# Outer gate taken as a per-token scale in the output evacuation, with exp of its logit folded into attention, and gate logits in four column tiles

## The chip, the cores and the metric

The kernel runs on one core of a Trainium2 chip. The metric is the device time of one execution in microseconds (us). Engines are named PE (TensorE matmul; PEld is its weight loading), DVE (VectorE), ACT (ScalarE), POOL (GpSimd) and SP (SyncE, which here only issues DMAs).

## The reference

```
x = A_x                                             # 2048 tokens x 512
g = sigmoid((x * gate_w).sum(-1, keepdims=True))    # one number per token
a = attention(x)     # 32 heads of 16, 4 segments of 512 tokens: causal softmax inside a
                     # segment, mixed with a linear-attention memory (phi, M, z) of the
                     # earlier segments by sigmoid(beta) per head; then @ wo
b = (gelu(x @ w_gate) * (x @ w_up)) @ w_down        # hidden size 1792
return g * a + (1 - g) * b
```

## The kernel before

The whole program is a list of tasks (`add`, `group`, `evac`), each with an engine (or a choice of two), a guessed cost, a priority and the tasks it depends on. A planner (`Sched.run`) walks through time with those guesses and emits the instructions of each engine in the order in which it would start them. The order on each engine is therefore fixed when the program is built, and a changed cost, dependency or task anywhere can move instructions that the edit does not mention, and can move an evacuation from DVE to ACT or back. `group` makes a PE task that fills a PSUM tile; `evac` makes the task that empties it. PSUM tiles come from two rings: "lg" (three tiles of 128x1024, for gate pairs and attention logits) and "gen" (two tiles of 128x512, for everything else). The planner also knows PE's tile modes: "row" (attention logits, four heads in four row strips), "col" (attention times values, four column strips) and "full". It charges 100 ns for a mode change and holds a "col" group back for up to 2.2 us unless a "row" group went just before it.

The work has two parts. The first, up to about 80 us, loads the weights, computes q, k and v of segment 0, and all the gate products of the geglu: `gate_pair` (28 of them, tile `gt`) multiplies x by 256 columns of w_gate and ACT applies gelu into `G`. `up_group` (56, tile `up`) multiplies by w_up, and DVE multiplies the PSUM result into `G`. Fourteen of the up groups (segment 0) lie in the first part, the others in the second. The second part is attention: 80 logit slots (`logit_slot`, tile `lg`), 160 exps on ACT, 160 causal selects on POOL, 32 products with the values (`pv_group`, tile `pv`), the memory (`phi`, `m_update`, `mem_den`, `mem_num`), and between the logit slots the fillers, among them the q, k, v of the next segment, the up groups, and `out_group`, which accumulates down projection and attention projection of 128 tokens in one PSUM tile (`dn`). After the last attention work four such groups are left to run alone.

The outer gate lives in `gate_row(s)`, once for each segment. `gwB` holds gate_w copied to 128 columns, so that four full matmuls of 512 columns (tile `gz`, line 452) give the logit of each token on all 128 partitions. ACT takes tanh of half of it (tile `th`, line 461). DVE makes from it `g1b` = 1 - g (line 464), which multiplies every pair of gate tiles after gelu (line 490), and, through a 32x32 block transpose (tile `tt`, line 469), `G2` = g with tokens on partitions (line 472). `G2` multiplies the reciprocal of the softmax sum (`f_rg`, line 665) and that of the memory's denominator (`f_g`, line 803). So g reaches the attention side and 1 - g the geglu side before both are added up in PSUM, and the evacuation of the sum (`osb`, through the helper `copy`, lines 181 and 183) is a plain copy.

The task that opens the pool of the attention tiles (`reopen`) depends on all gate pairs being multiplied and on `G2`; the pool `ph1` of the first part, which holds w_gate, `g1b`, `th` and `tt`, is closed there, and the attention tiles take its memory.

Of the kernel before, what the change touches and what calls it, by code (L numbers as in the profile page):

```python
# [8 lines left out]
AF = mybir.ActivationFunctionType  # L9
ALU = mybir.AluOpType  # L10
BF = dt.bfloat16
F32 = dt.float32

P = 128
# [141 lines left out]
def kernel(  # L156
# [22 lines left out]
    def copy(e, dst, src):  # L179
        if e == "ACT":  # L180
            nc.scalar.activation(dst, src, AF.Copy)  # L181
        else:
# [9 lines left out]
             "osb": 2, "th": 1, "tt": 1}  # L192
# [3 lines left out]
    def ctile(name, shape, dtype=BF):  # L196
        return cp.tile(shape, dtype, name=name, tag=name)
# [28 lines left out]
    gwB = ctile("gwB", [P, FC, P])  # L226
# [5 lines left out]
    G2 = ctile("G2", [P, NSEG, QB], F32)  # L232
    omg = ctile("omg", [P, NCH], F32)
# [16 lines left out]
    g1b = p1.tile([P, NSEG * L], BF, name="g1b", tag="g1b")  # L250
# [198 lines left out]
    def gate_row(s, prio):  # L449
        def mms(t):  # L450
            for fc in range(FC):
                nc.tensor.matmul(t[:, :], lhsT=gwB[:, fc, :], rhs=xT[:, fc, s * L:(s + 1) * L],
                                 start=(fc == 0), stop=(fc == FC - 1))
        gwt = TAB.get("gwB")
        g, box = group("gz", 4 * MM, mms, prio, [a_x[s], gwt])
        read_x[s].append(g)
        tl = {}

        def f_th(e, t):
            tl["th"] = rtile("th", [P, L], F32, p1)  # L460
            nc.scalar.activation(tl["th"][:, :], t[:, :], AF.Tanh, scale=0.5)

        def f_g1(e):
            nc.vector.tensor_scalar(out=g1b[:, s * L:(s + 1) * L], in0=tl["th"][:, :],
                                    scalar1=-0.5, scalar2=0.5, op0=ALU.mult, op1=ALU.add)

        def f_tt(e):
            tl["tt"] = rtile("tt", [P, QB, 32], F32, p1)
            nc.vector.transpose(tl["tt"][:, :, :].rearrange("p a b -> p (a b)"), tl["th"][:, :])

        def f_g2(e):
            nc.vector.tensor_scalar(out=G2[:, s, :], in0=tl["tt"][:, :, 0], scalar1=0.5,
                                    scalar2=0.5, op0=ALU.mult, op1=ALU.add)
        th = evac("ACT", g, box, f_th, alloc=["th"])
        g1 = add("DVE", 420, f_g1, deps=[th], prio=1, frees=[("th", th)])
        tt = add("DVE", 630, f_tt, deps=[th], prio=6, alloc=["tt"], frees=[("th", th)])
        g2 = add("DVE", 110, f_g2, deps=[tt], prio=6, frees=[("tt", tt)])
        TAB[("g1", s)], TAB[("g2", s)] = g1, g2

    def gate_pair(s, hp, prio):  # L480
        def mms(t):
# [8 lines left out]
        GM[(s, hp)] = add("DVE", 620, lambda e: nc.vector.tensor_mul(  # L490
            dst, dst, g1b[:, s * L:(s + 1) * L][:, None, :].to_broadcast((P, 2, L))),
            deps=[ge, TAB[("g1", s)]], prio=4)
# [10 lines left out]
    def f_gwB(e):  # L503
        for fc in range(FC):
            nc.vector.tensor_copy(gwB[:, fc, :], gw[:, fc:fc + 1].to_broadcast((P, P)))
    TAB["gwB"] = add("DVE", 1000, f_gwB, deps=[a_gw], prio=3)
# [26 lines left out]
    for s in range(NSEG):  # L533
        gate_row(s, 40 + 20 * s)
# [15 lines left out]
    opened = add("EXT", 0, reopen, deps=list(GM.values()) + [TAB[("g2", s)] for s in range(NSEG)])  # L550
# [71 lines left out]
    def pv_group(s, c, e):  # L622
# [58 lines left out]
        rg = add("DVE", 120, f_rg, prio=3, deps=[r, TAB[("g2", s)]])  # L681
# [185 lines left out]
    def out_group(s, qt, prio):  # L867
# [6 lines left out]
        def fn(e):  # L874
            bx["o"] = rtile("osb", [P, D])
            copy(e, bx["o"][:, :], box["t"][:, :])
        ev = add(["DVE", "ACT"], [610, 560], fn, prio=0, deps=[g], alloc=["osb"],
# [55 lines left out]
    for s in range(NSEG):  # L933
        for t in range(NSLOT):
            logit_slot(s, t)
            if TAB["first_x"] is None:
                TAB["first_x"] = XT_[(0, 0)]
            if t == 0:
                if s == 0 or True:
                    fillers(s)  # L940
# [38 lines left out]
```

## Time and profile before

| | |
|---|---|
| time, median of 3 runs | 293.13 us (293.1 to 293.29) |
| profiled execution, its own time | 292.86 us |
| its span | 291.2 us |
| PE busy | 274.3 us (94% of the span) |
| ACT busy | 210.6 us (72%) |
| DVE busy | 197.6 us (68%) |
| POOL busy | 126.5 us (43%) |
| PE clock granted | 0.999 of full speed |

The span runs from the first to the last instruction of the profiled execution; 1.66 us of its own time lie outside it. Busy time is the time in which at least one instruction of the engine is open. Matmuls are pipelined: in a stream of 512-column matmuls each lasts about 380 ns from start to end, but one starts every 216 ns.

### The profile page before, as it was taken

Reading aid. Unit: us, or ns where it says so; the run is one execution under the profiler, and the core shown is the slowest. Engines: PE = TensorE matmul, PEld = TensorE weight load, DVE = VectorE, ACT = ScalarE, POOL = GpSimd, SP = SyncE. Lnnn points to the kernel's source line nnn. Section 1 sums busy time; section 2 is a strip of 40 time slices with the busy share of each in tenths; the row PEclk is TensorE's granted clock in tenths of the full one; section 3 lists DMA queues with packets and bytes.
Section 4 is the critical chain, followed back from the end, with each engine's and each line's share of the span. In section 5 each row is a group of like instructions: output and inputs, shape, how many; then the busy total and the mean of one; then the engine's idle time right before and its main releaser. Section 6 shows DMA issues by size and latency. Waiting matters only on the chain.

```text
span 291.2 us, 5670 instructions
## 1 busy us (share of the span) xinstructions
PE 274.3 (94%) x2279; PEld 118.8 (41%) x2320; DVE 197.6 (68%) x355; ACT 210.6 (72%) x231; POOL 126.5 (43%) x188
## 2 busy tenths in 40 slices
PE   8999999999999979999998999988999999997994
PEld 3444444444434433443334444333444434333441
DVE  2331796554577898888999687699977865868400
ACT  3634664353399969899988999999998998985111
POOL 8000000000038674955478686564855864564000
PEclk9999999999999999999999999999999999999999
DMA  7975930000001130100002010000000000000011
GB/s 246 337 123 142 372 117 2 0 0 2 0 0 37 38 38 2 38 0 2 1 2 56 18 39 19 20 0 2 2 19 20 8 14 20 19 20 18 20 36 37
DMA packets 22019, 13.74 MB, mean 47 GB/s; under 512 B 14056, under 2 KB 20968, under 8 KB 21992
## 3 DMA queue, kind: packets, MB, share of 16 engines
q1 hardware_dynamic: 20392, 11.80, 14.8%
q10 hardware_dynamic: 1600, 1.57, 1.6%
q8 instruction: 18, 0.29, 0.4%
q14 instruction: 9, 0.07, 0.1%
HBM read 8.13 MB, written 2.10 MB: 35 GB/s over the span
## 4 chain that ended last, share of the span: by engine, by line
PE 73%; DVE 20%; DMA 3%; issue 1%; ACT 1%; ACTq 0%
PE gt L337 17%; PE dn L838 15%; PE up L337 14%; PE lg L582 6%; PE pv L634 6%; PE dn L843 4%; DMA wga<-in_B_w_gate_dram 3%; PE v L434 3%; PE q L337 3%; DVE T L652 3%; DVE N L670 2%; DVE G L499 2%; PE k L337 2%; DVE Nm L826 2%; DVE Tm L822 1%
## 5 line engine op out<-in xcount | busy, mean ns | idle before, releaser
L605 ACT ACTIVATE pT<-lg 128x1024 bf16<-128x1024 f32 x160 | 153.5, 1028 | 12.9 <-PE lg L582 12.3
L614 POOL TENSOR_SCALAR_AFFINE_SELECT pT<-pT 128x512 bf16<-128x512 bf16 (+1 forms) x160 | 94.3, 600 | 133.9 <-ACT pT L605 133.2
L499 DVE TENSOR_TENSOR G<-up,G 128x512 bf16<-128x512 f32 x56 | 38.3, 687 | 28.3 <-PE up L337 28.2
L337 PE MATMUL up<-xT,wup 128*128 128x512 bf16 x213 | 55.3, 380 | 1.1 <-DVE G L499 0.4
L838 PE MATMUL dn<-wdn,G 128*128 128x512 bf16 x213 | 52.3, 380 | 2.3 <-DVE T L652 1.3
L487 ACT ACTIVATE G<-gt 128x1024 bf16<-128x1024 f32 x28 | 28.7, 1024 | 33.9 <-PE gt L337 33.7
L337 PE MATMUL gt<-xT,wga 128*128 128x512 bf16 x217 | 51.3, 379 | 0.7 <-DMA wga<-in_B_w_gate_dram 0.3
L337 PEld LDWEIGHTS <-wga 128*128 128x128 bf16 x224 | 21.7, 98 | 26.8 <-DMA wga<-in_B_w_gate_dram 0.8
L838 PEld LDWEIGHTS <-G 128*128 128x128 bf16 x224 | 20.4, 98 | 27.1 <-issue 5.6
L337 PEld LDWEIGHTS <-wup 128*128 128x128 bf16 x224 | 20.0, 97 | 25.8 <-issue 5.6
L652 DVE STREAM_TRANSPOSE T<-pv 128x512 f32<-128x512 f32 x32 | 22.8, 711 | 10.9 <-PE pv L634 10.8
L490 DVE TENSOR_TENSOR G<-G,g1b 128x1024 bf16<-128x1024 bf16 x28 | 18.4, 685 | 2.1 <-ACT G L487 2.1
L181 ACT ACTIVATE osb<-dn 128x512 bf16<-128x512 f32 x9 | 5.4, 596 | 19.0 <-PE dn L843 19.0
L582 PE MATMUL lg<-qT,kO 32*128 32x128 bf16 (+2 forms) x320 | 18.1, 272 | 0.0
L582 PE MATMUL lg<-qT,kT 16*128 16x256 bf16 (+2 forms) x320 | 17.9, 273 | 0.1
L434 PE MATMUL v<-wv,xT 128*128 128x512 bf16 x61 | 15.5, 379 | 1.2 <-DVE vz_84 L183 0.5
L843 PE MATMUL dn<-wo,xT 128*128 128x512 bf16 x64 | 16.5, 380 | 0.1
L337 PE MATMUL q<-xT,wq 128*128 128x512 bf16 x60 | 15.8, 380 | 0.7 <-DVE kT L183 0.5
L582 PEld LDWEIGHTS <-kT 16*128 16x128 bf16 x320 | 7.1, 92 | 19.7 <-issue 19.2
L670 DVE TENSOR_TENSOR N<-T,r 128x512 bf16<-128x512 f32 x16 | 14.8, 926 | 0.3
L634 PE MATMUL pv<-pT,vz_84 128*32 128x256 bf16 (+2 forms) x320 | 11.7, 275 | 2.3 <-POOL pT L614 1.8
L582 PEld LDWEIGHTS <-kO 32*128 32x128 bf16 x320 | 7.1, 92 | 14.4 <-issue 14.1
(115 smaller groups left out, 270.3 us busy)
## 6 DMA issues: line engine op xcount, KB each, us to landing
out_dram<-osb SPq DMA_DIRECT2D x16, 128.0 KB, 1.7
wup<-in_B_w_up_dram SPq DMA_DIRECT2D x1, 1792.0 KB, 8.0
wdn<-in_B_w_down_dram SPq DMA_DIRECT2D x1, 1792.0 KB, 13.5
wga<-in_B_w_gate_dram SPq DMA_DIRECT2D x1, 1280.0 KB, 10.7
wq<-in_A_wq_dram SPq DMA_DIRECT2D x1, 512.0 KB
wga<-in_B_w_gate_dram ACTq DMA_DIRECT2D x1, 512.0 KB, 9.4
wv<-in_A_wv_dram ACTq DMA_DIRECT2D x1, 512.0 KB, 12.1
wo<-in_A_wo_dram SPq DMA_DIRECT2D x1, 512.0 KB, 9.1
```

The costliest lines, as they stand in the source:

```text
L337: nc.tensor.matmul(t, lhsT=W[:, fc, c0:c0 + P], rhs=xT[:, fc, s * L:(s + 1) * L], start=(fc == 0), stop=(fc == FC - 1))
L434: nc.tensor.matmul(t[:, :], lhsT=xT[:, fc, s * L + kt * P:s * L + (kt + 1) * P], rhs=wv[:, fc, :], start=(fc == 0), stop=(fc == FC - 1))
L487: ge = evac("ACT", g, box, lambda e, t: nc.scalar.activation(dst, t[:, :, :], AF.Gelu_apprx_tanh), cost=960, ring="lg")
L499: UPT[(s, hs)] = evac("DVE", g, box, lambda e, t: nc.vector.tensor_mul(G[:, s, hs, :], t[:, :], G[:, s, hs, :]))
L582: nc.tensor.matmul(A[j // 2][:, j % 2, at * P:(at + nq) * P], lhsT=l, rhs=r, start=True, stop=True, tile_position=(32 * j, 0))
L605: nc.scalar.activation(pT[(s, t, h)][:, :, :], A[h][:, :, :], AF.Exp, scale=0.25)
L614: nc.gpsimd.affine_select(out=v, in_=v, pattern=pat, compare_op=ALU.is_ge, fill=0.0, base=0, channel_multiplier=-1)
L634: nc.tensor.matmul(t[32 * j:32 * j + 32, qb * P:(qb + nq) * P], lhsT=vz[s % 2][:, kt, h * VW:h * VW + 32], rhs=pT[(s, t0 + w, j // 2)][:, ...
L652: nc.vector.transpose(TT[key][:, e, :, :].rearrange("p a b -> p (a b)"), t[:, :])
L670: nc.vector.tensor_mul(NN[key][:, :, :, :].rearrange("p a e d -> p e a d"), TT[key][:, :, :, 0:DH], RR[key][:, :, :, :].to_broadcast((P, 2 ...
L838: nc.tensor.matmul(t[:, :], lhsT=G[:, s, hs, qt * P:(qt + 1) * P], rhs=wdn[:, hs, :], start=(hs == 0), stop=stop and (hs == HS - 1))
L843: nc.tensor.matmul(t, lhsT=xT[:, c, s * L + qt * P:s * L + (qt + 1) * P], rhs=wo[:, c, :], start=first and c == 0, stop=(c == NCH - 1))
```

## The change

The sum g*a + (1-g)*b is rewritten as (1-g) * (e^z * a + b), where z is the gate's logit, since g/(1-g) = e^z. `G2` becomes e^z, and 1 - g = 1/(1 + e^z) becomes `omz`, a scale for each token that is applied where the finished sum leaves PSUM. The four `gate_row` become one `gate_rows`: `gwB` has 32 columns, and the four segments' logits are computed as four column tiles of one PSUM tile. DVE block-transposes that tile once; POOL spreads the result with 32 small copies over partitions into `G2` and `omz`; ACT takes exp of both, at a place after the first exp of attention; DVE finishes `omz`. The multiplication of `G` by `g1b` is gone, and with it `g1b`, `th` and the tanh. The task `gate_rows` is put ahead of the gate pairs of segment 3, and `reopen` now depends on the gelus and on POOL's copies.

```diff
-    gwB = ctile("gwB", [P, FC, P])
+    gwB = ctile("gwB", [P, FC, 32])
...
+    omz = ctile("omz", [P, NSEG, KT], F32)
...
-    g1b = p1.tile([P, NSEG * L], BF, name="g1b", tag="g1b")
...
-    def gate_row(s, prio):
+    def gate_rows(prio):
         def mms(t):
             for fc in range(FC):
-                nc.tensor.matmul(t[:, :], lhsT=gwB[:, fc, :], rhs=xT[:, fc, s * L:(s + 1) * L],
-                                 start=(fc == 0), stop=(fc == FC - 1))
...
+                for s in range(NSEG):
+                    nc.tensor.matmul(t[32 * s:32 * s + 32, :], lhsT=gwB[:, fc, :],
+                                     rhs=xT[:, fc, s * L:(s + 1) * L], start=(fc == 0),
+                                     stop=(fc == FC - 1), tile_position=(0, 32 * s),
+                                     skip_group_check=True)
+        g, box = group("gz", 4 * MM, mms, prio, a_x + [TAB["gwB"]], mode="col")
...
-            nc.scalar.activation(tl["th"][:, :], t[:, :], AF.Tanh, scale=0.5)
...
-            nc.vector.tensor_scalar(out=g1b[:, s * L:(s + 1) * L], in0=tl["th"][:, :],
-                                    scalar1=-0.5, scalar2=0.5, op0=ALU.mult, op1=ALU.add)
...
-            nc.vector.tensor_scalar(out=G2[:, s, :], in0=tl["tt"][:, :, 0], scalar1=0.5,
-                                    scalar2=0.5, op0=ALU.mult, op1=ALU.add)
...
+            nc.vector.transpose(tl["tt"][:, :, :].rearrange("p a b -> p (a b)"), t[:, :])
+
+        def f_sp(e):
+            z = tl["tt"]
+            for s in range(NSEG):
+                src = slice(32 * s, 32 * s + 32)
+                for j in range(4):
+                    dst = slice(32 * j, 32 * j + 32)
+                    nc.gpsimd.tensor_copy(G2[dst, s, :], z[src, :, 0])
+                    nc.gpsimd.tensor_copy(
+                        omz[dst, s, :],
+                        z[src, :, :].rearrange("p (kt a) b -> p a kt b", a=4)[:, j, :, 0])
+
+        def f_ex(e):
+            nc.scalar.activation(G2[:, :, :], G2[:, :, :], AF.Exp)
+            nc.scalar.activation(omz[:, :, :], omz[:, :, :], AF.Exp)
+
+        def f_om(e):
+            nc.vector.tensor_scalar_add(omz[:, :, :], omz[:, :, :], 1.0)
+            nc.vector.reciprocal(omz[:, :, :], omz[:, :, :])
...
+        tt = evac("DVE", g, box, f_tt, alloc=["tt"])
+        TAB["zsp"] = add("POOL", 4000, f_sp, deps=[tt], prio=6, frees=[("tt", tt)])
+
+        def later():
+            TAB["g2"] = add("ACT", 500, f_ex, deps=[TAB["zsp"], TAB["first_x"]], prio=2)
+            TAB["omz"] = add("DVE", 250, f_om, deps=[TAB["g2"]], prio=5)
...
-        GM[(s, hp)] = add("DVE", 620, lambda e: nc.vector.tensor_mul(
-            dst, dst, g1b[:, s * L:(s + 1) * L][:, None, :].to_broadcast((P, 2, L))),
-            deps=[ge, TAB[("g1", s)]], prio=4)
+        GM[(s, hp)] = ge
...
-        gate_row(s, 40 + 20 * s)
+        if s == 3:
+            gate_rows(40 + 20 * s)
...
-            copy(e, bx["o"][:, :], box["t"][:, :])
-        ev = add(["DVE", "ACT"], [610, 560], fn, prio=0, deps=[g], alloc=["osb"],
+            g = omz[:, s, qt:qt + 1]
+            if e == "ACT":
+                nc.scalar.activation(bx["o"][:, :], box["t"][:, :], AF.Copy, scale=g)
+            else:
+                nc.vector.tensor_scalar_mul(bx["o"][:, :], box["t"][:, :], g)
+        ev = add(["DVE", "ACT"], [610, 560], fn, prio=0, deps=[g, TAB["omz"]], alloc=["osb"],
```

## The prediction

> **What bounds the kernel now.** I read the busy table first, then busy time by stretch, then the chain that ended last, then single instructions.
>
> ```profile
> PE 274.3 (94%) x2279; PEld 118.8 (41%) x2320; DVE 197.6 (68%) x355; ACT 210.6 (72%) x231; POOL 126.5 (43%) x188
> ...
> 40.00:60.00 20.00, 19.89 (x92) 9.11 (x93) 12.44 (x26) 9.06 (x10) 0.00 (x0) 1.00 0.01 1
> 60.00:80.00 20.00, 19.89 (x95) 8.90 (x94) 10.75 (x18) 7.83 (x9) 0.00 (x0) 1.00 0.00 1
> ...
> 100.00:120.00 20.00, 17.26 (x176) 7.64 (x172) 18.73 (x35) 16.57 (x19) 12.91 (x17) 1.00 0.17 27
> 120.00:140.00 20.00, 19.05 (x204) 7.79 (x205) 16.79 (x29) 18.73 (x21) 12.83 (x21) 1.00 0.04 9
> 140.00:160.00 20.00, 18.07 (x212) 7.79 (x213) 19.37 (x35) 17.78 (x20) 13.88 (x19) 1.00 0.08 21
> ```
>
> The stretches give length, then PE, PEld, DVE, ACT, POOL busy. From 40 to 80 us PE is never idle while DVE and ACT are about half idle: this part is bound by PE alone, and a DVE microsecond there is worth nothing. In the second part PE, DVE and ACT are all near full, and from 100 to 120 and 140 to 160 us PE loses 2.7 and 1.9 us to DVE. The chain (start, length, what) says the same. Three pieces of it are the gate logits:
>
> ```profile
> 30.69 1.73 PE gz L452 x8
> ...
> 42.77 0.86 PE gz L452 x4
> ...
> 61.77 0.86 PE gz L452 x4
> ...
> 79.93 1.03 ACT G L487
> 80.99 0.69 DVE G L490
> 81.68 0.61 DVE G L499
> ```
>
> So the logits stand on the path with all their 3.45 us, and of the 28 multiplications of line 490 only the last stands on it. The PE sequence of the second part is what sets its end, with DVE as the engine it most often waits for.
>
> **What the Trainium skill says.** (1) "TensorE: Matmul & The Clock Gate", Part 3: matmuls in distinct column strips run concurrently; three measured 2.38 times faster. The trace agrees with more: a `pv` group is 20 matmuls in four strips, five rounds of four with 1280 columns in all per strip, and the next full matmul starts 0.67 us after the group does; its 5120 columns in turn, at 0.216 us for 512, would take 2.2 us.
>
> ```profile
> 266.89 3.18 PE L838 MATMUL dn<-wdn,G 128*128 128x512 bf16 x13 [1.30 <-DVE T L652]
> 270.00 0.73 PE L634 MATMUL pv<-pT,vz_85 128*32 128x512 bf16 x20
> 270.67 1.04 PE L843 MATMUL dn<-wo,xT 128*128 128x512 bf16 x4
> ```
>
> (2) "TensorEngine Tiling (Array Packing)", Key Properties: a change of tiling mode drains the array. The three lines price it, full to column and back. The last `dn` matmul started 0.38 us before the modelled end, 270.07; the next full one could have started 0.216 us after it, at 269.91; `pv` starts at 270.00, so entry costs 0.09. Its 1280 columns take 1280/512 x 0.216 = 0.54 of the 0.67 us, so leaving costs 0.13. Together 0.22 us. (3) "GPSIMD Engine Reference", Specifications: POOL contends with DVE instructions that have two SBUF inputs. The trace has it (start, length):
>
> ```profile
> 103.26 2.56 DVE L670 TENSOR_TENSOR N<-T,r 128x512 bf16<-128x512 f32 x1
> ...
> 103.16 2.12 POOL L708 TENSOR_TENSOR pkT<-E,Q_1013 128x1024 bf16<-128x1024 bf16 x1
> ```
>
> The 16 `N` average 0.93 us, and an undisturbed one (272.15) took 0.69.
>
> **The change part by part.**
>
> Gate logits on PE. Gone: 16 full matmuls x 0.216 = 3.46 us, all on the path. Added: 4 rounds of 4 concurrent matmuls of 512 columns, 4 x 0.216 = 0.86, plus the mode change 0.22, = 1.08 us. Gain 2.38 us. The instruction orders of the two programs show it as one block of 16 between full gate pairs, six up groups and six gate pairs before the first logit; nothing but PE's own sequence holds it. The bounds: if strips did not overlap at all, 3.46 + 0.22, a loss of 0.2.
>
> Gate multiplication and its inputs on DVE and ACT (lines 461, 464, 469, 472, 490). Gone: 28 x 0.685 = 19.2 us, 4 x 0.425, three of four transposes at 0.71 and 4 x 0.17 on DVE, 4 x 0.594 on ACT. All but the last multiplication lie beside PE work in the first part, cover being PE at 19.89 of 20 us; they are worth nothing. The last one: the second k group at 82.34 waited 0.28 us for the up evacuation behind it. The up matmuls end at 81.2 anyway, so I take 0.2, bounds 0 and 0.3. What is late next there is the table load of ACT (80.97, 1.28 us), unchanged; both programs have three.
>
> The new transpose of `gz` from PSUM: 0.71 us (the row of line 652) on a half idle DVE; nothing waits for it but POOL. The next up evacuation stands behind it, 2.6 us apart from its predecessor. Nothing.
>
> POOL's 32 copies, of 16 or 4 elements on 32 partitions. No row shows one. The nearest, a memset and a select of four elements per partition (lines 286 and 287), took 0.095 and 0.195, the select of 8x128 0.33. I take 0.2 x 32 = 6.4 us; from 3 to 11. The block of logits ends 72 matmuls (15.6 us) before the first logit slot, about 62 us, and the transpose by 63. ACT asks for `G2` after four attention activations, 5 us after its table load, about 83. That leaves 20 us, 0.6 us for each copy. POOL has nothing else to do from 20 us to there (busy 0.00), so this costs nothing; what waits behind it would be POOL's first select and ACT's exps.
>
> Two small exps on ACT, 64 and 16 elements: the activations of 1024 (1.028) and 512 elements (0.596) give 0.16 + 0.84 ns each, so 0.22 + 0.18 = 0.4 us, early in the attention. The plan moves two other evacuations from ACT to DVE there (nine left of eleven before the tail), so ACT loses 1.2 us of work against that. Two small DVE operations, 0.17 + 0.18 us (lines 518, 517). I set these at nothing net; bounds -0.4 and +0.4.
>
> Output evacuations. Same count, one scale more. Of 16, ACT did 9 and does 6, DVE 7 and now 10. The only one with no cover is the last (287.34, ACT): "ScalarE: Activation LUTs", What ACT_TABLE_LOAD costs, gives about 93 ns for each per-partition operand; the trace of before has no such activation. I take +0.09; bounds 0 and 0.1. DMAs are as before in number, size and order.
>
> Order. This is the unknown. From about 213 us on, the PE order is the same to the end. Between 80 and 213 the up groups, `pv` and memory groups stand in another order; the mode changes go from 193 to 195, both of the new ones being the logit block's. By stretches of 5 us, PE's idle time from 100 to 215 us sums to 8 us. A changed order can win some of that or add as much again. For: in the new DVE order, the first `N` stands ahead of the `min` that releases the `pkT` addition which it collided with. Against: the plan that gives the new order does not know of such collisions, and other ones can arise. I take 0, bounds -2.5 and +4.
>
> Sum: -2.38 - 0.2 + 0.09 = -2.5 us. Against the profiled execution's 292.86 this gives 290.4. The median of the runs shown lies 0.27 higher, at 293.13, so 290.6 there; I state **290.5**, with its own range 289.3 to 291.6.
>
> **The rivals.**
>
> (a) The order helps as well. The collision at 103.26 cost 1.9 us of DVE, and `pv` then waited 1.8 us for POOL's selects at 106.48, behind the same `pkT`. If it goes and nothing takes its place: 290.5 - 2 = 288.5, down to 287.5 if a second such hole (155 to 160 us, PE busy 3.84 of 5) closes too.
>
> (b) Slower: VectorE and GpSimd collide more often in the new order. Place: 95 to 160 and 190 to 210 us, where DVE is 69 to 100% busy in every stretch of 5 us and its queue holds the evacuations of the two "gen" tiles that PE needs next. Price: 1.9 us of DVE each time a two-input operation meets a `pkT` or `pq` addition. Twelve such additions exist, so there is room. One more collision on the path leaves 292.4; from two (3.8 us against 2.5) the change is lost, at 294.4; three give 296. Against it: DVE's amount of work there is the same but for two evacuations (1.4 us).
>
> (c) The column tiles do not overlap: 293.1. `pv` speaks against it.
>
> (d) POOL's copies cost over 0.6 us each: at 1 us they end 12 us after ACT needs them, which gives 302. No row supports it.
>
> **How the numbers follow.** Chances: as forecast 0.55, (a) 0.23, (b) 0.14, (c) 0.04, (d) 0.04. A measurement of this kernel can tell about 0.2%, 0.6 us, from no change. Faster by more than that: the first two and a little of (b), 0.80; within it (c) and the edge of (b), 0.05; slower 0.15. For 8 in 10 the range runs from 287.6, which leaves the far end of (a) out, to 294.0, which takes in (c), one added collision of (b) and the upper bounds of the small costs, and leaves out most of (b) and (d).
>
> **What would show each step.** The `gz` matmuls in one block of about 1.1 us near 61 us; the first logit about 2.4 us earlier, near 77.4 instead of 79.83; no line 490; POOL's 32 copies ending before 75 us with no ACT wait on POOL behind them; three table loads; the last output evacuation near 0.69 us; and the distance from the first logit to the end of the span within 1.5 us of the 211.4 of before. The forecast is wrong if the first logit does not come earlier by 2 us, or if that distance grows by over 2 us; then the DVE waits of PE between 95 and 210 us show where.

## The result

The changed kernel takes **295.14 us** (median of 4 runs, 294.87 to 295.24) against 293.21 us for the kernel before beside it (4 runs, 293.1 to 294.15): ratio 1.0057, 95% interval 1.0035 to 1.0079. It is slower by 1.9 us between these medians and by 1.7 us by the ratio, where 2.5 us less were forecast. Its profiled execution took 295.16 us with a span of 293.5 us. One line of the result explains much of what follows: the mean clock granted to TensorE was 0.991 to 0.994 in all four runs, and 0.999 in the profiled execution of before. Where the clock is halved for one stretch of 3.41 us, the mean over 293 us falls by 0.006; what that stretch is, is told below.

The busy table and the stretches of the profile after, with the same columns as before (length, then PE, PEld, DVE, ACT, POOL busy, granted clock):

```profile
PE 274.3 (93%) x2279; PEld 118.4 (40%) x2320; DVE 178.9 (61%) x320; ACT 208.7 (71%) x227; POOL 129.3 (44%) x220
```

```profile
60.00:80.00 20.00, 19.89 (x105) 8.67 (x106) 5.91 (x9) 7.97 (x8) 5.20 (x32) 1.00 0.00 1
100.00:120.00 20.00, 17.62 (x158) 7.51 (x160) 18.65 (x33) 17.63 (x19) 13.78 (x19) 1.00 0.21 34
120.00:140.00 20.00, 19.45 (x234) 8.14 (x235) 16.94 (x31) 17.96 (x20) 12.14 (x19) 1.00 0.01 2
140.00:160.00 20.00, 18.29 (x183) 7.79 (x186) 17.71 (x33) 18.50 (x22) 14.34 (x19) 1.00 0.06 15
```

DVE has lost 18.7 us of work, and the span has grown by 2.3: the work was where DVE was half idle. From 100 to 160 us PE is even a little busier than before. These tables show no loss, so it has to be looked for in places that a 20 us average hides.

The first part did what the forecast said. The chain (start, length, what):

```profile
61.50 0.98 PE gz L454 x16
62.47 0.97 PE up L337 x4
...
78.12 0.33 PE lg L594 x4
78.44 0.97 PE up L337 x4
79.41 1.81 PE k L337 x8
```

The sixteen logit matmuls are one block of 1 us, line 490 is gone from the chain, and the eight `k` matmuls run unbroken. From the first gate product to the first logit PE took 68.52 us before (11.31 to 79.83) and takes 66.19 now (11.86 to 78.05): 2.33 us less.

What was lost comes after the first logit. The distance from there to the end of the span was 211.3 us and is 215.4. Split by the starts of the 160 exps (two for each logit slot) and of PE's last `dn` matmul:

| stretch | before, us | after, us | difference |
|---|---|---|---|
| first logit to first exp | 2.44 | 2.44 | 0 |
| first exp to eleventh | 13.47 | 14.40 | +0.93 |
| eleventh exp to last | 169.66 | 170.03 | +0.37 |
| last exp to last `dn` matmul | 21.48 | 24.15 | +2.67 |
| last `dn` matmul to the end | 4.27 | 4.39 | +0.12 |

Two places hold nearly all: the first ten exps and the stretch behind the last one. The first, PE's and DVE's and POOL's instructions at 85 us (start, length, engine, line, and in brackets PE's wait and what ended it):

```profile
84.36 0.69 DVE L183 CAST vz_85<-v 128x512 bf16<-128x512 f32 x1
84.59 2.12 POOL L720 TENSOR_TENSOR pkT<-E,Q_742 128x1024 bf16<-128x1024 bf16 x1 [0.74 <-DVE E L716]
84.96 1.78 DVE L481 TENSOR_SCALAR omz<-omz 128x16 f32<-128x16 f32 x1
...
86.78 0.25 DVE L482 RECIPROCAL omz<-omz 128x16 f32<-128x16 f32 x1
86.95 1.22 DVE L183 CAST vz_85<-v 128x512 bf16<-128x512 f32 x2
```

```profile
87.63 1.02 PE L434 MATMUL v<-wv,xT 128*128 128x512 bf16 x4 [1.14 <-DVE vz_85 L183]
88.59 0.40 PE L594 MATMUL lg<-qT,kO 32*128 32x512 bf16 x4
```

Line 481 is `omz + 1`, sixteen elements for each partition, and takes 1.78 us. It ends at 86.74, 0.03 us after POOL's `pkT` addition (86.71). Two `v` evacuations stand behind it, PE waits 1.14 us for a "gen" tile, and the next logit slot comes behind that.

The second, PE's last waits, in the profiled execution of the table:

```profile
263.89 0.73 PE L646 MATMUL pv<-pT,vz_85 128*32 128x512 bf16 x20
265.34 0.38 PE L825 MATMUL num<-pq,Mbd 128*128 128x512 bf16 x1 [0.72 <-DVE osb L892]
267.39 4.87 PE L850 MATMUL dn<-wdn,G 128*128 128x512 bf16 x13 [1.67 <-DVE T L664]
272.19 0.73 PE L646 MATMUL pv<-pT,vz_85 128*32 128x512 bf16 x20
```

In before, `num` followed `pv` without a wait, `dn` waited 1.30, and its 13 matmuls took 3.18 us:

```profile
264.37 0.73 PE L634 MATMUL pv<-pT,vz_85 128*32 128x512 bf16 x20
265.22 0.38 PE L813 MATMUL num<-pq,Mbd 128*128 128x512 bf16 x1
```

Now the two waits are 0.72 and 1.67, the gap from the end of `pv` to `dn` is 2.8 us where it was 1.8, and the same 13 matmuls take 4.87. The stretches show why (length, PE busy, ..., granted clock):

```profile
264.70:268.12 3.42, 1.05 (x4) 0.46 (x5) 3.35 (x6) 1.23 (x2) 1.27 (x2) 1.00 0.11 38
268.12:271.53 3.41, 3.41 (x10) 1.19 (x9) 0.55 (x1) 0.00 (x0) 0.00 (x0) 0.50 0.00 0
```

After a stretch with PE busy 1.05 us of 3.42, the clock is halved for 3.41 us. This "half clock" costs 1.7 us, the longer gap 1.0. Some executions of one kernel meet this half clock and some don't, so that each result below also tells how many did (a mean clock under 0.995; half clock in the last microseconds of the span, when PE has no work left, costs nothing and leaves the mean at 0.997 or more). Of the kernel before it was 38 of 193 over all comparisons (two more, of 458 and 953 us, are left aside), with a median of 294.58 us against 293.42 for the other 155. The mean doesn't tell where in an execution the clock fell. In the profiles of the changed kernel, of e9 and of e11 it is the place shown here; no profile of the kernel before caught one, and its place there stays open.

### The profile page after: what moved, and what is told of

Same layout as the page of the kernel before. It is cut to its first block, busy times and chain, and to the rows that moved or that the text cites. A ratio compares the mean times of both kernels' runs of the same rounds, so it can differ in the third digit from the quotient of the medians.

```text
span 293.5 us, 5671 instructions
## 1 busy us (share of the span) xinstructions
PE 274.3 (93%) x2279; PEld 118.4 (40%) x2320; DVE 178.9 (61%) x320; ACT 208.7 (71%) x227; POOL 129.3 (44%) x220
## 4 chain that ended last, share of the span: by engine, by line
PE 68%; DVE 20%; DMA 3%; issue 2%; ACT 2%; POOL 2%; ACTq 0%
PE gt L337 16%; PE dn L850 15%; PE up L337 13%; PE lg L594 6%; PE pv L646 5%; PE dn L855 4%; DMA wga<-in_B_w_gate_dram 3%; DVE T L664 3%; PE q L337 2%; PE k L337 2%; PE v L434 2%; DVE G L510 2%; DVE Nm L838 2%; DVE Tm L834 2%; ACT pT L617 2%
## 5 line engine op out<-in xcount | busy, mean ns | idle before, releaser
L626 POOL TENSOR_SCALAR_AFFINE_SELECT pT<-pT 128x512 bf16<-128x512 bf16 (+1 forms) x160 | 92.5, 587 | 73.7 <-ACT pT L617 72.9
L850 PE MATMUL dn<-wdn,G 128*128 128x512 bf16 x213 | 53.7, 389 | 3.5 <-DVE T L664 1.7
L471 POOL COPY G_90<-tt 32x16 f32<-32x16 f32 x16 | 3.1, 195 | 56.7 <-DVE tt L463 56.0
L890 ACT ACTIVATE osb<-dn,omz 128x512 bf16<-128x512 f32 x6 | 4.1, 686 | 20.8 <-PE dn L855 20.8
L594 PE MATMUL lg<-qT,kT 16*128 16x256 bf16 (+2 forms) x320 | 18.5, 273 | 0.1
L682 DVE TENSOR_TENSOR N<-T,r 128x512 bf16<-128x512 f32 x16 | 14.0, 875 | 0.3
L892 DVE TENSOR_SCALAR osb<-dn,omz 128x512 bf16<-128x512 f32 x10 | 7.5, 745 | 9.2 <-PE dn L855 6.7
```

What stands on the lines that cost most here:

```text
L594: nc.tensor.matmul(A[j // 2][:, j % 2, at * P:(at + nq) * P], lhsT=l, rhs=r, start=True, stop=True, tile_position=(32 * j, 0))
L626: nc.gpsimd.affine_select(out=v, in_=v, pattern=pat, compare_op=ALU.is_ge, fill=0.0, base=0, channel_multiplier=-1)
L682: nc.vector.tensor_mul(NN[key][:, :, :, :].rearrange("p a e d -> p e a d"), TT[key][:, :, :, 0:DH], RR[key][:, :, :, :].to_broadcast((P, 2 ...
L850: nc.tensor.matmul(t[:, :], lhsT=G[:, s, hs, qt * P:(qt + 1) * P], rhs=wdn[:, hs, :], start=(hs == 0), stop=stop and (hs == HS - 1))
```

## The experiments

Three theories were tried one after the other: the half clock, the new order of the second part, and the operations that the change adds. 

### Is the half clock the loss?

**e1** and **e2** keep PE busy in the gap, with matmuls that nothing reads, in the changed kernel and in the one before.

```diff
+    def f_fill(_):
+        t = lgtile("warm")
+        for i in range(8):
+            nc.tensor.matmul(t[:, 0, :], lhsT=wdn[:, 0, 0:P], rhs=wdn[:, 0, :],
+                             start=True, stop=True)
+    wf = add("PE", 1, f_fill, prio=0, deps=[TAB[("num", 3, 3)]], alloc=["lg"])
...
```

> The changed kernel with eight idle 512-column matmuls put on TensorE behind the last memory product, where it stood waiting from 265.7 to 267.4 us; nothing else is moved and nothing waits for them. Theory (half clock): the 1.0 us that TensorE idles longer at this place makes the clock drop to half for 3.4 us right behind it, which costs 1.7 us; with the matmuls in the gap the clock stays full and the time falls from 295.1 to about 293.4. Rival (order): the loss sits in the order between 80 and 260 us and in the late VectorE chain, the clock only accompanies it: the time stays within 0.5 us of 295.1.

> The kernel before with the same eight matmuls at the same place. It is the control for the first run: the clock was full there before, the gap was 1.3 us, and the matmuls need 1.7, so the half-clock theory expects no gain and at most 0.4 us of loss (293.1 to 293.6). If filling a gap helps for another reason, this one gains as well.

Measured: e1 293.81 us (14 runs, all at full clock; ratio to before 1.0008, 0.9995 to 1.002), e2 293.65 (14 runs, one below full clock; 0.9994, 0.998 to 1.0008). The half clock is real and goes when PE is kept at work, but without it the changed kernel is only level with before: the whole forecast gain of 2.5 us is still missing.

**e6** asks from the other side. In the kernel before, four memsets on DVE (1.45 us together) make the transpose late that the first of the last `dn` groups waits for.

```diff
         def f_T(_, t):
+            if key == (NSEG - 1, NCH - 1) and e == 0:
+                for _i in range(4):
+                    nc.vector.memset(gwB[:, :, :], 0.0)
```

> The kernel before with four memsets (about 1.0 us together, of a tile that is no longer read) on VectorE ahead of the transpose that frees the PSUM tile of the next-to-last output group, so TensorE waits there about 2.3 instead of 1.3 us. Theory (half clock, by a threshold of idle time): the delay of 1.0 us makes the clock drop for 3.4 us, and the time grows by 2.5 to 2.9 us. Rival (the drop needs something else of the changed kernel): the clock stays full and the time grows by 1.0 us.

Measured: 296.24 us (19 runs; 1.0078, 1.0059 to 1.0096). PE waited 2.72 us instead of 1.30:

```profile
265.79 0.38 PE L816 MATMUL num<-pq,Mbd 128*128 128x512 bf16 x1
268.89 3.18 PE L841 MATMUL dn<-wdn,G 128*128 128x512 bf16 x13 [2.72 <-DVE T L655]
```

Five runs at full clock had a median of 294.88, the delay alone; 14 at half clock had 296.42. A longer gap here is paid one for one (1.45 us put in, 1.46 between the medians at full clock), and it raised the share of executions that meet the half clock from a fifth to three quarters. The expected 2.5 to 2.9 us more came out (2.6), but as a mixture: not every execution meets it.

### Is it the order?

**e3** gives the changed kernel the order and engines that the kernel before has in its second part, and **e5** gives the kernel before the order of the changed one; both list the emission by hand in place of the planner (`ORDER`, one entry for each task).

> The changed kernel, with the order and the engines of the second part (from the first logit on) taken from the plan of the kernel before; the first part, the new operations and their places stay. Theory (order): of the 1.78 us by which the first logit came earlier, 1.3 us are lost by the last exp because of the new order; with the old order the lead of 1.8 to 2.3 us holds up to the last exp, at 263.1 to 263.6 us from the span's start. What the tail then does depends on whether the clock drops: 291.0 to 291.5 with full clock, 292.7 to 294 with half. Rival (bound elsewhere): the second part gives the lead back in any order because VectorE sets its pace; the last exp comes at 264.9 as in the changed kernel.

> The kernel before, with the order and the engines of the second part taken from the plan of the changed kernel; everything else, the four gate rows, the gate multiplication and the plain copies too, as before. Theory (order): the stretch from the first exp to the last grows by 1.1 to 1.3 us (183.1 before, 184.2 with the new order and plain copies), the clock stays full because plain copies keep VectorE in time, and the kernel takes 1.0 to 1.4 us more than before. Rival (the order is harmless and the loss comes from the new operations in the second part): within 0.4 us of before.

Measured: e3 292.01 us (7 runs, one at half clock; 0.9945, 0.9926 to 0.9965), e5 293.48 (22 runs, all at full clock; 0.9992, 0.998 to 1.0003). So the changed kernel gains about 3 us from the old order (half a microsecond less than expected), and the old kernel loses nothing by the new one. The order as such is harmless; the expectation for e5 was wrong. What the new order costs must lie in what the changed kernel alone has in it: the two small operations and the scaled evacuations. In e3 the small operation started 0.9 us ahead of POOL's addition (83.53 against 84.42) and took 0.18 us.

### The small operation

**e9** is the changed kernel with every order as it was, except that `f_om` stands ahead of the fourth up evacuation that follows the `v` evacuations. **e10** puts the same two operations, on a tile that nothing else reads, into e5 at the place where the changed kernel has them.

```diff
...
+    def f_om(e):
+        nc.vector.tensor_scalar_add(omz[:, :, :], omz[:, :, :], 1.0)
+        nc.vector.reciprocal(omz[:, :, :], omz[:, :, :])
...
+    TAB["om"] = add("DVE", 250, f_om, deps=[TAB["gwB"]], prio=5)
```

> The changed kernel with every engine's order as it was, except that VectorE's two small operations on omz stand six instructions of evacuation later, ahead of the fourth up evacuation after the v evacuations, where VectorE was idle for 0.6 us and GpSimd is past its additions. Theory (the small operation, which took 1.78 us beside a GpSimd addition where it stood, holds up the evacuations of v and with them the first logit slots): it takes 0.2 us now, the first ten exp slots take about 13.8 us instead of 14.40, and all that follows is 0.5 to 0.7 us earlier. The gap of TensorE before the last output groups is not touched, so the half clock for 3.4 us stays: about 294.5 us, last dn about 288.5. Rival (the slots lag for another reason, the small operation is only where it shows): the first ten slots stay at 14.3 to 14.5, the time at 295.1.

> The kernel before in the second part's order of the changed one, which ran at 293.48 us, and in it two operations on a tile of 128x16 that nothing else reads (a tensor_scalar and a reciprocal on VectorE), put where the changed kernel has them. Nothing of the computation changes. Theory (small operation beside GpSimd's addition): the first of them takes about 1.8 us, the first ten exp slots 14.3 to 14.5 us instead of 13.77, and the time is 0.5 to 0.7 us up, 294.1 with full clock, up to 295.5 if it also sets off the half clock at the end. Rival (a small operation costs what its size says): 0.2 us, 13.8 us and 293.5.

Measured: e9 293.77 us (22 runs; 1.0011, 0.9998 to 1.0024), e10 295.12 (6 runs, all at full clock; 1.0061, 1.0048 to 1.0075). Where it stands clear of POOL's additions (e9), and where it doesn't (e10):

```profile
91.26 0.50 DVE L466 TENSOR_SCALAR omz<-omz 128x16 f32<-128x16 f32 x1
```

```profile
87.28 2.12 POOL L707 TENSOR_TENSOR pkT<-E,Q 128x1024 bf16<-128x1024 bf16 x1 [0.91 <-DVE E L703]
...
87.66 1.77 DVE L544 TENSOR_SCALAR omz<-omz 128x16 f32<-128x16 f32 x1
```

The first ten exps took 13.41 us in e9 (14.40 in the changed kernel) and 14.77 in e10 (13.77 in e5): 1.0 us taken away and 1.0 put in, by one instruction of sixteen elements. In e9 it took 0.50 us, not the 0.2 expected; a POOL select had started 0.16 us ahead of it. The mechanism was as expected, and its size had been put at little over half: the total moved by 1.1 us in e9, against e13 below, and by 1.6 in e10. The profiled executions of e10 and e5 differ by 1.0 only (294.72 and 293.74), all of it in those exps; the rest of the 1.6 was not located. The half clock stayed in e9 (10 of 22 runs), as the theory had it.

### The scaled evacuations

**e4** is the changed kernel with plain copies in place of the scaled evacuations, which leaves the factor 1 - g out of the output.

```diff
-            g = omz[:, s, qt:qt + 1]
-            if e == "ACT":
-                nc.scalar.activation(bx["o"][:, :], box["t"][:, :], AF.Copy, scale=g)
-            else:
-                nc.vector.tensor_scalar_mul(bx["o"][:, :], box["t"][:, :], g)
+            copy(e, bx["o"][:, :], box["t"][:, :])
```

> The changed kernel with plain copies as the output evacuations, so the factor 1-g is left out; the order is unchanged. Theory (half clock, by a threshold): the ten scaled evacuations on VectorE (0.745 against 0.673 us each) and the last one on ScalarE (0.69 against 0.60) are worth 0.1 us at the end and some 0.1 in front of the last values product; the clock drop stays, 294.9 to 295.1. Rival (the scale is what made VectorE late): over 0.5 us is gained, and the clock drop is gone.

Measured: 292.68 us (22 runs, all at full clock; 0.9965, 0.9954 to 0.9977). More than the evacuations' own length went: the gap from the end of `pv` to `dn` ahead of the last groups fell from 2.8 us to 1.8, the 1.8 of the kernel before, and the half clock went with it, so the rival was right. By groups (count, then busy, mean ns) the scaled evacuation is 0.07 us longer on DVE than the plain copy of before, and 0.09 longer on ACT. In before:

```profile
L181 ACT ACTIVATE osb<-dn 128x512 bf16<-128x512 f32 x9 | 5.4, 596 | 19.0 <-PE dn L843 19.0
...
L183 DVE CAST osb<-dn 128x512 bf16<-128x512 f32 x7 | 4.7, 673 | 4.1 <-ACT pT L605 2.1 <-PE dn L843 2.0
```

In the changed kernel:

```profile
L892 DVE TENSOR_SCALAR osb<-dn,omz 128x512 bf16<-128x512 f32 x10 | 7.5, 745 | 9.2 <-PE dn L855 6.7 <-ACT pT L617 2.4
...
L890 ACT ACTIVATE osb<-dn,omz 128x512 bf16<-128x512 f32 x6 | 4.1, 686 | 20.8 <-PE dn L855 20.8
```

Do the two costs add up, what is left when both are gone, and does every execution of the changed kernel meet the half clock? **e13** is the changed kernel unedited, **e14** has the edits of e9 and e4 together, **e15** those of e3 and e4 (both leave 1 - g out of the output).

> The changed kernel once more, unedited, for more executions of it. Theory (the gap of TensorE before the last output groups lies close to what sets off the half clock, so that some executions meet it and some not): a mixture, most of them at a clock of 0.991 to 0.994 near 295.0 and some at full clock near 294.0, median 294.4 to 295.1. Rival (the gap of 2.8 us sets it off always): all at 0.991 to 0.994, 295.1.

> The changed kernel with both costs taken away: the small operations on omz later, as before, and the output evacuations plain copies (the scale by 1-g is left out of the output). Theory (the two are separate costs): 292.7 with plain evacuations less 1.2 to 1.4 us, which is 291.3 to 291.5, full clock. Rival (both reach the end through the same wait, so that only one of them can be won): 292.3 to 292.7.

> The changed kernel in the order of the kernel before in the second part, as in the run that took 292.01 us, and with plain output evacuations (the scale by 1-g is left out). What remains of the change is the first part (logits in column tiles, no multiplication by 1-g) and the two small exps. Theory (the first part gives the 2.4 us of the forecast, and in this order the scale costs 0.5 to 1 us): 291.1 to 291.5, full clock. Rival (the first part gives less, about 1.4 us, and the scale costs nothing in this order): 291.9 to 292.1.

Measured: e13 294.85 us (22 runs; 1.0035, 1.0019 to 1.005), 11 runs at full clock with a median of 294.23 and 11 at half clock with 295.40. e14 291.51 (6 runs; 0.9927, 0.9906 to 0.9947) and e15 291.4 (6 runs; 0.9918, 0.9897 to 0.9939), all at full clock. All three went as the theory said:

| | small operation beside `pkT` | moved (e9, e14) | difference |
|---|---|---|---|
| scaled evacuations | 294.85 (e13) | 293.77 | 1.1 |
| plain evacuations | 292.68 (e4) | 291.51 | 1.2 |
| difference | 2.2 | 2.3 | |

The two costs are independent within the noise. With both gone, the new order (e14) and the old (e15) differ by 0.1 us, and the rest of the change stands 2.0 us below the 293.42 of before at full clock. The scale's cost depends on the order, though: in the old one, where DVE has seven of the sixteen evacuations and not ten, it is about 0.6 us (292.01 in e3 against 291.4).

How do ten evacuations of 0.07 us more on DVE, and six of 0.09 on ACT, become 2.2 us? **e16** takes the scale from the last evacuation on DVE alone, the one at 264.55 us that PE waits for; **e17**, with the condition turned round, from all others.

```diff
...
+            NOUT.append(e)
+            if e == "DVE" and NOUT.count("DVE") == 10:
+                copy(e, bx["o"][:, :], box["t"][:, :])
...
```

> The changed kernel with a plain copy in one output evacuation, the last that VectorE does (264.55 us in its profile); its scale by 1-g is left out. Theory (VectorE reaches that place late from what came before, and the addition behind that evacuation then starts after GpSimd's next select instead of ahead of it, so that 0.07 us less there is too little): the gap of TensorE before the last output groups stays over 2.5 us, some executions still at half clock, 294.3 to 294.8. Rival (the one evacuation on the path decides): the gap falls to 1.85 us, full clock, 292.9 to 293.4.

> The complement: the last output evacuation that VectorE does keeps its scale, the other fifteen are plain copies (the scale by 1-g is left out in those). Theory (the sum of the earlier ones makes VectorE late): the gap falls to 1.9 us, full clock, 292.7 to 293.1. Rival (that one decides): the gap stays over 2.5 us and the time at 294.0 to 294.8.

Measured: e16 295.0 us (22 runs, 12 at half clock; 1.0035, 1.0019 to 1.0051), no gain; e17 292.79 (22 runs, all at full clock; 0.9973, 0.9962 to 0.9983), all of the gain. The evacuation on the path is not the cause; the other fifteen are. What they do is seen in who comes first, DVE's `N` + `Nm` addition or POOL's next select. In the changed kernel:

```profile
264.55 0.74 DVE L892 TENSOR_SCALAR osb<-dn,omz 128x512 bf16<-128x512 f32 x1
265.09 0.63 POOL L626 TENSOR_SCALAR_AFFINE_SELECT pT<-pT 128x512 bf16<-128x512 bf16 x1 [1.00 <-ACT pT L617]
265.21 0.78 DVE L687 TENSOR_TENSOR N<-N,Nm 128x512 bf16<-128x512 bf16 x1
```

and with plain evacuations (e14):

```profile
263.01 0.68 DVE L168 CAST osb<-dn 128x512 bf16<-128x512 f32 x1
263.61 0.41 DVE L674 TENSOR_TENSOR N<-N,Nm 128x512 bf16<-128x512 bf16 x1
...
264.09 0.64 POOL L613 TENSOR_SCALAR_AFFINE_SELECT pT<-pT 128x512 bf16<-128x512 bf16 x1 [0.73 <-ACT pT L604]
```

Measured from ACT's last pair of exps (263.99 and 263.00), the addition starts 1.22 us behind it in the first and 0.61 in the second. DVE, late against ACT and POOL, falls behind the select and takes 0.78 us instead of 0.41; in e16 it is still behind (265.22 after 265.15, 0.84 us), in e17 ahead (265.86 before 266.28, 0.41 us). That the lateness comes from the other evacuations is shown by e16 and e17.

It is not the sum of all of them, by the profiles. Laid over e4's profile, with the first exps together, DVE's instructions in the changed kernel start where e4's do, to within 0.02 us, up to the evacuation at 230.6 us: what the six evacuations ahead of it took longer has gone into DVE's waits. That one, the one at 250.6 and the one at 257.5 us then put DVE 0.18 us behind. This is enough to turn round a first meeting, DVE's `Nm` product (line 838) with a select. In the changed kernel:

```profile
259.45 0.64 POOL L626 TENSOR_SCALAR_AFFINE_SELECT pT<-pT 128x512 bf16<-128x512 bf16 x1 [0.28 <-ACT pT L617]
259.60 1.03 DVE L838 TENSOR_TENSOR Nm<-Tm,rm 128x512 bf16<-128x512 f32 x1
```

and in e4:

```profile
260.26 1.20 POOL L626 TENSOR_SCALAR_AFFINE_SELECT pT<-pT 128x512 bf16<-128x512 bf16 x1 [0.28 <-ACT pT L617]
260.34 0.63 DVE L838 TENSOR_TENSOR Nm<-Tm,rm 128x512 bf16<-128x512 f32 x1
```

In e4 it is the select that takes twice as long, and `Nm` goes through (starts this close, 0.08 and 0.15 us apart, don't tell who holds whom; the lengths do). After it the changed kernel is 0.59 us behind, after a second `Nm` (263.79 us, 0.83 us against 0.69) and the last evacuation 0.80, and after the `N` + `Nm` addition 1.17. So 0.18 us of longer evacuations becomes 1.0 us of gap for PE by three lost meetings with selects, and the gap brings the half clock. No run set one of the three evacuations apart.

### The gap itself, and a faster kernel

**e7**, **e8** and **e12** fill the gap with useful work: the output groups of the last segment accumulate in logit tiles, which are free by then, and their down products wait only for the last logits, while the attention product keeps the old dependencies. e7 does it to the changed kernel, e8 to e3, e12 to the kernel before.

```diff
-                    box["t"] = gen("dn")
+                    box["t"] = gen("dn") if ring == "gen" else lgtile("dn")[:, 0, :]
...
+        end = s == NSEG - 1
+        ring = "lg" if end else "gen"
+        att = [t_wo] + [OTT[(s, c)] for c in range(NCH)]
         first, prev, box = pieces(s, qt, prio, False,
-                                  [t_wo] + [OTT[(s, c)] for c in range(NCH)])
+                                  [LT[NSEG * NSLOT - 1]] if end else att, ring)
...
-                deps=[prev])
+                deps=[prev] + (att if end else []))
```

> The changed kernel, where the four output groups of the last segment accumulate in logit tiles, free once the last logits are there, and their down products no longer wait for the attention result (only the projection does), so real work of TensorE can stand in the gap at the tail. Theory (idle gap and half clock): the 1.7 us of half clock and most of the 2.4 us of idle time go: 3 to 4 us faster than the changed kernel, 1 to 2 us faster than before. Rival (the chain of VectorE up to the last transpose sets the end in any case): under 2 us faster than the changed kernel.

> Both: the changed kernel with the order of before in the second part and the last output groups in logit tiles. If order and tail are separate losses, their gains add up: 1.6 us under before from the third run, and the 1.3 to 1.5 us of the gap at the tail on top, so 2.6 to 3.2 us faster than before, 290.0 to 290.6 where before has 293.2. If the new order lost its time only through the tail, this is no faster than the run without the old order.

> The kernel before with the four output groups of the last segment in the logit ring, their down products waiting only for the last logits, as in the run of the changed kernel with this edit, which gained 2.8 us. Theory (1.7 of those 2.8 us were the half clock, which the kernel before mostly does not meet; the rest is the gap before the last output groups, which it has too): the gap of 1.85 us between the last mem_num product and the down products is filled, gain 0.8 to 1.2 us, 292.3 to 292.8, at full clock. Rival (all that edit did was to keep the clock up): 293.3 to 293.6.

Measured: e7 292.33 us (6 runs; 0.9932, 0.9906 to 0.9958; 2.5 to 2.8 us below the changed kernel, where 3 to 4 were expected), e8 **290.55** (6 runs, one at half clock; 0.9876, 0.985 to 0.9902), e12 291.95 (15 runs; 0.9946, 0.9928 to 0.9963). PE in e8, where before it waited 1.30 and in the changed kernel 2.4:

```profile
264.54 0.38 PE L812 MATMUL num<-pq,Mbd 128*128 128x512 bf16 x1
264.85 0.73 PE L633 MATMUL pv<-pT,vz 128*32 128x512 bf16 x20
265.74 3.19 PE L837 MATMUL dn<-wdn,G 128*128 128x512 bf16 x14 [0.16 <-issue]
```

e12 gained 1.6 us, more than the 0.8 to 1.2 expected, and only one of its 15 runs met the half clock. e8 beats both kernels; set against e12, the change is then worth 1.4 us.

### The start

**e11** asks why the first gate product came 0.55 us later in the profile after. The change makes `gwB` narrower, so that all tiles behind it have other addresses; here it is padded, and 32 of its columns are used.

```diff
-    gwB = ctile("gwB", [P, FC, 32])
+    gwB = ctile("gwB", [P, FC, 120])
```

> The changed kernel with gwB 120 columns wide instead of 32, of which 32 are used, so that every SBUF tile after it, w_gate's among them, has the address that it has in the kernel before. The question is why the first gate product starts at 11.6 to 12.2 us in the six profiles of kernels with the change and at 11.0 to 11.3 in the four without. Theory (the address at which the first slice of w_gate lands matters for the transfers): it starts at 11.0 to 11.3, and the time is 294.6. Rival (addresses do not matter): 11.6 to 12.2, and 295.1.

Measured: 294.45 us (11 runs, 4 at half clock; 1.0026, 1.0008 to 1.0044), first gate product at 11.70 us. The addresses are not it. Nor is the change: e10 and e12, built on the kernel before, had 11.70 and 11.57. The first gate product, which waits for w_gate's transfer, came at 10.96 to 12.21 us over all profiles. What moves it stays open; it means that half a microsecond between two single profiles of the first part says nothing.

## Why the prediction was wrong

**Right: the logit block.** 3.46 us to 1.08 by the forecast. By the last five full matmuls ahead of the block (from 60.25, one each 0.216 us) the next could have started at 61.33; it started at 62.41, which is 1.08 us. The first part became 2.33 us shorter against the 2.38 worked out (the medians over all profiles, 13 with the block and 6 without, differ by 2.2), and e15, which keeps this part alone, gained 2.0 us in the median. The tiles overlap, as rival (c) denied.

**Right: line 490, the transpose and POOL's copies.** The wait of 0.28 us for the second `k` group is gone. The copies took 0.18 to 0.20 us each, 5.8 us in all, and ended at 69.1, twelve microseconds ahead of POOL's first select; rival (d) had no ground:

```profile
63.30 0.19 POOL L471 COPY G_90<-tt 32x16 f32<-32x16 f32 x1 [56.04 <-DVE tt L463]
...
68.93 0.19 POOL L472 COPY omz<-tt 32x4 f32<-32x4 f32 x1
```

**Right: the last evacuation.** 0.69 us, +0.09; the two exps on ACT took 0.27 and 0.22 us against 0.4 together.

**Right in value: the order at 0.** e5 and the pair e14, e15 put it at -0.2 to +0.1 us. It was a middle taken between -2.5 and +4, so the value is luck as much as insight, and what the change adds costs more in the new order than in the old.

**The first step that failed: "Two small DVE operations, 0.17 + 0.18 us", set at nothing net with bounds of 0.4.** They took 1.78 and 0.25 us and cost 1.1 us at the end. The prediction had half of the rule in hand: it priced a collision of DVE with POOL's `pkT` addition at 1.9 us, and rival (b) was built on it. But it applied the rule to instructions that the new order moves, and to operations with two SBUF inputs alone, and priced the new one by its size. The Trainium skill's page "SBUF — State Buffer", section "SBUF: two separate sides", says that the ports shared by the two engines are held exclusively for a whole instruction, so that the later one is blocked fully, and that a VectorE operation in a two-port mode needs them too, not only one with two SBUF inputs, which is all that the prediction's third reading names. The trace agrees with the first (the operation ended 0.03 us after POOL's addition, in the changed kernel and in e10); no run shows in which mode it ran.

**The second: "The only one with no cover is the last" of the output evacuations.** The scale on the others cost 2.2 us. Up to 230 us the cover was there, and nothing of the scale is left in DVE's starts; the last three ahead of 264 us had too little of it, the instructions behind them lost their place ahead of POOL's selects, and the lateness comes out ahead of the last output groups, where PE has nothing else to do. The prediction had counted ten scaled evacuations on DVE and given none of them a price, on an engine that it had itself named as the one PE most often waits for.

**What it did not have at all: the clock.** A gap ahead of the last groups was visible in before (1.30 us of waiting). The mean clock of 0.999 was no sign of it: there the clock was halved for the last 0.53 us of the span, when PE had no work left. That a gap of another microsecond halves the clock for 3.4 us in about half of the executions was in no rival; it is worth 1.2 us between the two kinds of execution in e13 (0.9 in e9, 1.5 in e6, 1.8 in e16), 0.6 in the median of many runs, and the whole 1.2 in the four runs of the result.

The sum as the runs put it: -2.0 for the first part, +1.1 for the small operation, +2.2 for the scales with the half clock that they bring, +1.3 us in all; e13 measured 294.85 - 293.71 = +1.1. Rival (b) gave 294.4 and was near in the number, and its mechanism, VectorE against GpSimd, is what happened at both places. But its instructions were others, at the end it was POOL's selects that they met and not the twelve additions that it counted, its price of 1.9 us for each was the time on DVE and not on the path, and it held only 0.14. The prediction's own test, a distance from first logit to end grown by over 2 us, caught the failure (4.1), and pointed to the waits between 95 and 210 us, where there is little of it: one loss lies at 85 us and the other at 264.

## What to carry to other kernels

A small instruction put on a busy engine is priced by what it can collide with where it will stand, not by its size: look up what the neighbour engine runs at that moment, and place it by hand in a hole. When an operation that recurs gets longer by a tenth on an engine that others wait for, look for the places where it has no wait to disappear in and where it can lose its turn against a neighbour engine; the instruction on the path there may be innocent. And before giving a gap of the matrix engine a price, see whether it lies next to the point from which the clock falls: independent work that can be pulled into the gap is then worth more than the gap.

## What the runs showed of the hardware

**The clock falls by windows.** In every profile the stretches at one clock, from the first at full clock on, last whole multiples of 3.413 us (in the changed kernel 77 at full, 1 at half, 6 at full), and the first begins at a phase of its own, 3.9 to 7.1 us after the span's start. So each profile has a grid of windows. The Trainium skill, "TensorE: Matmul & The Clock Gate", Part 1, tells of a free-running window of 3413 ns and of a half clock after an idle one. The trace agrees with the window but not with idle: PE was busy 1.05 us in the window ahead of the half clock in the changed kernel, 0.96 in e9 and 1.70 in e11. The same gap in e13's profile was cut in two by the grid, and the clock stayed full:

```profile
262.63:266.05 3.42, 2.46 (x39) 1.10 (x37) 3.39 (x6) 3.02 (x4) 1.45 (x3) 1.00 0.00 0
266.05:269.46 3.41, 1.97 (x10) 0.90 (x10) 2.65 (x5) 0.00 (x0) 0.64 (x1) 1.00 0.11 38
```

Over all windows of all 19 profiles up to the end of the span, the ten with PE busy for 1.33 us or less were followed by half clock, and those with 1.36 or more by full clock (1.36 in e6, 1.68 in e16, 1.78 at 102.9 us in before), with one exception, the 1.70 of e11. That window is full of small matmuls that overlap: counted by columns, at 0.216 us for 512, it had 1.19 us, and the one of e6 1.20. An estimate of the limit from these is 1.2 us of 3.413; one window of e8 (1.16 by columns at 101.9 us, full clock after it) doesn't fit, and no run set the limit on purpose. That the phase decides is a reading of the profiles and was not tried by itself; it would explain why one program has executions 1.2 us apart. The gap at the end need not be the only place: in before's profile the emptiest window ahead of the end is the one at 102.9 us, with 2.16 at the last groups, and e2 and e12, where those are filled, still had one execution each under 0.995.

**A tensor_scalar of 128x16 took 0.18 us alone (e3) and 1.78 us beside a GpSimd addition**, 0.50 beside a select (e9), while a cast from PSUM beside the same addition kept its 0.68 us (e3, 84.78 us).

**Of two that meet, one pays.** Of a VectorE product of two SBUF tensors and a GpSimd select that start 0.08 to 0.15 us apart, one kept its length and the other took 0.4 to 0.6 us more: the product in the changed kernel (1.03 and 0.64 us), the select in e4 (0.63 and 1.20).

**A per-partition scale in an evacuation of 128x512** cost 0.07 us on DVE (673 to 745 ns) and 0.09 on ACT (596 to 686 ns).
